# Clamped block additions, a square over three blocks, a second kind of group with seven products, and other tile starts

## The chip, the cores and the metric

The kernel runs on one core of one Trainium2 chip. The metric is the time of one execution on the device in microseconds (us). TensorE (PE in the profile) multiplies matrices; its weight loads are listed apart as PEld. VectorE (DVE) and ScalarE (ACT) work on elements, GpSimd (POOL) and SyncE (SP) issue DMA transfers here. The program gives each engine its own queue of instructions, in a fixed order.

## The reference

Two stages. Attention over channels: for each of 4 batches, q, k and v have 6080 tokens of 256 channels; q and k are normalised over the tokens, the 256 x 256 matrix of products of their channels goes through a softmax, and v is multiplied by it. Then a feed-forward block with 2048 hidden channels and the square of a relu:

```python
s = kn.transpose(0, 2, 1) @ qn / tau
a = softmax(s)                      # over the last axis
x = (v @ a).reshape(B * N, 256)
h = np.maximum(x @ w_in, 0.0)
return (h * h @ w_out).astype(np.float32)
```

## The kernel before

**Forms of the weights.** The softmax matrix is folded into `w_in` once per batch, so the main work is h = W.v and then out = w_out.h^2 for each block of tokens. Everything is held as a high and a low part (`_hi`, `_lo`) of the reduced type fp32r, and each product is three matmuls: hi with hi, hi with lo, lo with hi. The part that is streamed through the array is the "moving" operand: v and the parts of h^2.

**Blocks and groups.** A batch has 12 token blocks: ten of 512 tokens and two of 480, each used as two halves (256 or 240). The first two blocks of the run and the last one go another way. The 45 between them make 180 groups: four per block, j = 0 to 3, each with 512 of the hidden channels, that is two pairs of 256. `period(k)` writes out the work of group k. In a group both matrix products are done in the manner of Strassen and Winograd, on blocks of 2 x 2: seven block products instead of eight, with sums of blocks in place of the eighth.

- First product: `product` issues seven block products (42 matmuls) into the PSUM banks B2, H and C (`ps_b`, `ps_h`, `ps_c`). ScalarE copies or clamps them into the tile `x`, with blocks a0, a1, a3, a2 in this order, and VectorE adds what H and C hold to a1 and a3. The bank C starts as ScalarE's copy of B2, and PE then adds the product `C, S2` to it; so PE must wait for that copy.
- Square: before, a0 is clamped on the way out of PSUM and squared by ScalarE (`square`); a1 and a3 are added by VectorE and then clamped and squared by VectorE in one pass (`relu_squares`); a2 is clamped and squared by ScalarE.
- Sums: `first_sum`, `second_sum`, `third_sum` and `last_sum` on VectorE make the sums of blocks that the second product needs. `hi_A`/`lo_A` and `hi_S`/`lo_S` split them into parts (ScalarE makes the high part, VectorE the low one). The A tiles hold a1, a3, a2 and the S tiles (`s1`, `s2`; one name `s` in the profile) a0 with a1 and a3 with a2.
- Second product: `to_output` adds into the two output tiles `ps_o`, in three windows, `window_A`, `window_S(..., "S1")` and `window_S(..., "S2")`, of which the last falls into the period after next.

**Plain groups.** `plain(k)` tells whether the second pair of a group is done with eight block products instead of seven (its sums are then not taken, and each sum and its parts cover one pair instead of two). j=0 is always plain, j=2 and j=3 never after the first block, and j=1 is plain in all batches but the last: that is what `EARLY` and `LATER` say. For the seven products of a second pair, sums of blocks of `w_out` are needed, which `other_sums_of_w_out` makes for the j of EARLY around the first groups, and for those of LATER just before the last batch.

**Beside it.** While one batch runs, generators insert the next batch's attention at fixed points (`side("dve")`, `"pe"`, `"act"`, `"mid"`): one chunk of q and k per period, split into `qk_hi` and `qk_lo`, squared and added up, then the softmax, then the new forms of W. In the last batch there is nothing to insert. `v_step` splits the next token block's v at j=1 and j=2.

**Tiles.** The pools lay their tiles one behind another in SBUF. The two tiles `qk_lo` and `qk_hi` stand ahead of those of v (`v`, `v_hi`, `v_lo`) and of the S parts (`s_hi`, `s_lo`), and behind the A parts. Eight unused numbers at the end of each half make each of the two 64 bytes longer per partition than its content.

```python
EARLY = (2, 3)
LATER = (1,)
def plain(k):
    b, n, j = groups[k]
    return not (j in EARLY and (b, n) != order[OLD] or j in LATER and b == B - 1 and n >= LATER.index(j))
```

Of the kernel before, what the change touches and what calls it, by code (L numbers as in the profile page):

```python
# [7 lines left out]

F32 = mybir.dt.float32
# [5 lines left out]
ALU = mybir.AluOpType  # L15
# [15 lines left out]
def kernel(  # L31
# [484 lines left out]
    def attention(b):  # L516
# [21 lines left out]
        for c in range(c0, g.n):  # L538
            yield from until("act")
            if c > c0:  # L540
                g.squares(c - 1)
            p, jn, _ = g.q[c]
            hi = pool.tile([P, 2, J * C + 8], F32R, tag="qk_hi", name=f"qk_hi{b}_{c}", bufs=1)
            lo = pool.tile([P, 2, J * C + 8], F32R, tag="qk_lo", name=f"qk_lo{b}_{c}", bufs=1)
            hi, lo = (x[:, :, 0 : J * C].rearrange("p a (j c) -> p a j c", j=J) for x in (hi, lo))
            h_, l_, r_ = (x[:p, :, :jn, :] for x in (hi, lo, g.raws[c]))
            scalar.copy(h_, r_)
            yield
            yield from until("mid")
            add_and_load(c - 1)  # L550
            yield
            yield from until("dve")
            vector.tensor_sub(l_, r_, h_.bitcast(F32))
            yield
            yield from until("pe")
            for _ in g.products(c, [(hi, hi), (hi, lo), (lo, hi)]):
                pass
            yield
# [358 lines left out]
    BS = (B - 1,)  # L917
    EARLY = (2, 3)
    LATER = (1,)
    order = [(b, n) for b in range(B) for n in range(NB)]  # L920
# [37 lines left out]
    def half_of(k):  # L958
        return blocks[groups[k][1]][1] // 2
# [151 lines left out]

    def relu_squares(k):
        s = XG[k][:, :, a1 : a3 + 1, :]
        vector.scalar_tensor_tensor(s, s, 0.0, s, op0=ALU.max, op1=ALU.mult)

    def square(k, at):
        s = XG[k][:, :, at, :]
        scalar.activation(s, s, AF.Square)
# [76 lines left out]
    def period(k, before=nothing, w1=None, wa=None, w3=None):  # L1195
# [48 lines left out]
        product(k, H, S4, B22)  # L1244
        s = x[:, :, a1, :]
        vector.tensor_add(s, s, H[:, :, :half])
        if prev and not plain(k - 1):
            last_sum(k - 1)
        product(k, C, S3, T3)
        s = x[:, :, a3, :]  # L1250
        vector.tensor_add(s, s, C[:, :, :half])
        if prev:
            lo_S(k - 1, "S1")
            hi_S(k - 1, "S2")
        square(k, a0)
        relu_squares(k)
        if prev:
# [13 lines left out]
        evict_C21(k)  # L1271
        square(k, a2)
        if not after_copy(k):
# [217 lines left out]
```

## Time and profile before

| what | value |
|---|---|
| median of 3 runs | 2150.75 us (2150.54 to 2152.3) |
| profiled execution, from its first to its last instruction | 2150.0 us |
| granted TensorE clock | 1.000 |
| groups 0 to 178 | from 158.3 us to 2088.6 us of that execution |
| moved by DMA | 552.19 MB, mean 257 GB/s |

All instructions that the program issues through its recording wrapper carry one line number (L27), so the groups of the profile are told apart by the names of their tiles, out<-in, with the numbers left out: `ps_c<-v_hi,wf` is a product of the forms of W with v into the bank C. A row of the table of groups gives the count, the busy time and the mean duration of one. Durations on ScalarE and VectorE overlap a little: the next instruction starts about 0.1 us before the last one's recorded end.

The chain of work that ended last runs over TensorE for 90% of the span, over VectorE for 6% and over ScalarE for 1%.

### The profile page before, as it was taken

To read this page: it belongs to the slowest core of one execution; us is meant where nothing else is said; L and a number is where in the kernel's file an instruction comes from. 1 tells how busy PE (TensorE), PEld (TensorE's weight loads), DVE (VectorE), ACT (ScalarE), POOL (GpSimd) and SP (SyncE) were. 2 spreads that over 40 slices of the span, in tenths; PEclk is the share of its full clock that TensorE was granted. 3 is DMA by queue.
4 is the path that set the end of the run, shared out by engine and by line. 5 is a ranking of instruction groups with operands and counts; after the bars stand their busy time and mean duration, and the time that the engine had idled before them with its cause. 6 is when DMAs were issued, how large, how long until landed. Compare 5 with 4: busy or idle time off the path is not lost.

```text
span 2150.0 us, 44018 instructions
## 1 busy us (share of the span) xinstructions
PE 2139.5 (100%) x16990; PEld 2081.8 (97%) x16990; DVE 1973.7 (92%) x2739; ACT 1726.7 (80%) x2550; POOL 441.1 (21%) x561
## 2 busy tenths in 40 slices
PE   9999999999999999999999999999999999999999
PEld 8789999999999999999999999999999999999998
DVE  6899999999998999999999999999999999999993
ACT  5887888778878888877878888877887877877875
POOL 0000221212222221222122221221222222222221
PEclk9999999999999999999999999999999999999999
DMA  9777788879999988877999988887999788788783
GB/s 349 229 234 267 241 255 252 228 227 296 305 291 266 294 245 254 239 236 245 306 302 277 310 246 249 248 245 218 330 325 289 227 233 244 231 233 243 232 245 89
DMA packets 259986, 552.19 MB, mean 257 GB/s; under 512 B 27568, under 2 KB 120752, under 8 KB 259776
## 3 DMA queue, kind: packets, MB, share of 16 engines
q1 hardware_dynamic: 191488, 448.01, 61.8%
q0 software_dynamic: 68288, 101.35, 22.7%
q8 instruction: 134, 2.20, 0.4%
q14 instruction: 76, 0.62, 0.1%
HBM read 430.97 MB, written 63.70 MB: 230 GB/s over the span
## 4 chain that ended last, share of the span: by engine, by line
PE 90%; DVE 6%; DMA 1%; ACT 1%; issue 1%; SPq 0%; POOL 0%; DVEq 0%; ACTq 0%
PE ps_o L27 40%; PE ps_c L27 16%; PE ps_h L27 13%; PE ps_b L27 11%; PE gram L27 6%; DVE x L27 3%; PE ps_w L27 2%; DVE s_lo L27 1%; PE ps_o_m L27 1%; DVE A_lo L27 1%; DMA o<-o 1%; ACT x L27 1%; DMA qk<-in_q 0%; DVE v_lo L27 0%; DMA w_raw_hi<-in_w_in 0%
## 5 line engine op out<-in xcount | busy, mean ns | idle before, releaser
L27 DVE TENSOR_TENSOR s_lo<-x,s_hi 128x1024 fp32r<-128x1024 f32 (+1 forms) x384 | 463.4, 1207 | 37.8 <-ACT s_hi L27 37.7
L27 ACT CAST s_hi<-x 128x1024 fp32r<-128x1024 f32 (+1 forms) x384 | 400.8, 1044 | 96.7 <-DVE x L27 87.1
L27 PE MATMUL ps_c<-v_hi,wf 128*128 128x256 f32 (+1 forms) x2160 | 469.9, 281 | 3.3 <-DVE x L27 2.2
L27 POOL DMA_DIRECT2D o<-o x225 | 250.2, 1279 | 986.3 <-ACT o L27 612.0
L27 DVE TENSOR_TENSOR x<-x 128x512 f32<-128x512 f32 (+3 forms) x720 | 406.3, 564 | 15.7
L27 PEld LDWEIGHTS ps_c<-v_hi,wf 128*128 128x128 f32 x2160 | 369.1, 189 | 6.7 <-DVE x L27 3.5
L27 ACT CAST A_hi<-x 128x1024 fp32r<-128x1024 f32 (+3 forms) x360 | 247.2, 687 | 89.6 <-DVE x L27 81.4
L27 PE MATMUL ps_b<-v_hi,wf 128*128 128x256 f32 (+1 forms) x1440 | 311.8, 280 | 0.0
L27 PE MATMUL ps_h<-v_hi,wf 128*128 128x256 f32 (+1 forms) x1440 | 311.4, 279 | 0.0
L27 PE MATMUL ps_c<-v_lo,wf 128*128 128x256 f32 (+1 forms) x1080 | 301.9, 280 | 0.0
L27 DVE TENSOR_TENSOR A_lo<-x,A_hi 128x1024 fp32r<-128x1024 f32 (+3 forms) x360 | 275.5, 765 | 2.2 <-ACT A_hi L27 1.4
L27 ACT ACTIVATE x<-x 128x512 f32<-128x512 f32 (+3 forms) x384 | 251.8, 656 | 6.1
L27 PEld LDWEIGHTS ps_b<-v_hi,wf 128*128 128x128 f32 x1440 | 245.9, 189 | 0.1
L27 PEld LDWEIGHTS ps_h<-v_hi,wf 128*128 128x128 f32 x1440 | 245.8, 189 | 0.0
L27 ACT COPY x<-ps_c 128x512 f32<-128x512 f32 (+1 forms) x180 | 104.9, 583 | 168.3 <-PE ps_c L27 168.1
L27 DVE SCALAR_TENSOR_TENSOR x<-x 128x1024 f32<-128x1024 f32 (+1 forms) x180 | 217.3, 1207 | 0.0
L27 PE MATMUL ps_o<-s_hi,wo_hi 128*128 128x256 f32 (+3 forms) x1009 | 207.9, 296 | 0.5 <-ACT s_hi L27 0.5
L27 PE MATMUL ps_o<-s_lo,wo_hi 128*128 128x256 f32 (+3 forms) x1009 | 207.7, 296 | 0.1
L27 PE MATMUL ps_o<-s_hi,wo_lo 128*128 128x256 f32 (+3 forms) x1009 | 207.8, 296 | 0.0
L27 PEld LDWEIGHTS ps_c<-v_lo,wf 128*128 128x128 f32 x1080 | 203.8, 189 | 0.1
L27 PE MATMUL ps_h<-v_lo,wf 128*128 128x256 f32 (+1 forms) x720 | 201.5, 280 | 0.0
L27 PE MATMUL ps_b<-v_lo,wf 128*128 128x256 f32 (+1 forms) x720 | 201.2, 279 | 0.0
(165 smaller groups left out, 5113.5 us busy)
## 6 DMA issues: line engine op xcount, KB each, us to landing
wf<-wf_kept SPq DMA_DIRECT2D x360, 512.0 KB, 5.5
wf<-wf_kept SPq DMA_DIRECT2D x360, 384.0 KB, 5.0
o<-o POOLq DMA_DIRECT2D x114, 256.0 KB, 6.9
qk<-in_k SPq DMA_DIRECT2D x87, 256.0 KB, 5.1
qk<-in_q SPq DMA_DIRECT2D x87, 256.0 KB, 5.3
out_T<-o POOLq DMA_DIRECT2D x152, 128.0 KB, 5.3
v<-in_vT POOLq DMA_DIRECT2D x76, 128.0 KB, 3.8
v<-in_vT POOLq DMA_DIRECT2D x38, 256.0 KB, 4.1
```

What stands on the lines that cost most here:

```text
L27: return lambda *args, **kwargs: self.tc.keep_in_program_order(issue(*args, **kwargs))
```

## The change

It has three parts.

1. `EARLY = (1, 2, 3)`, `LATER = ()`: the groups j=1 of all blocks but the first use seven products for both pairs. 33 groups are concerned, those of batches 0 to 2; in batch 3 they did so already.
2. VectorE's two additions from PSUM clamp at zero in the same instruction (`add_relu`, a custom instruction that gives max(min(in0 + in1, s0), s1) with s0 infinite and s1 zero). VectorE's pass `relu_squares` goes, and ScalarE squares the blocks a0, a1 and a3 in one instruction.
3. The eight unused numbers in the `qk` tiles go. In the built program the v and S tiles then begin 128 bytes earlier, at multiples of 256 bytes instead of 128 past one; the A tiles stay where they were, at a multiple of 256.

```diff
@@ -5,6 +5,7 @@
 from concourse import mybir
 from concourse.masks import make_identity
 from concourse._compat import with_exitstack
+from concourse.dve_ops import TENSOR_ADD_SAT
 
 F32 = mybir.dt.float32
 F32R = mybir.dt.float32r
@@ -540,9 +541,9 @@
             if c > c0:
                 g.squares(c - 1)
             p, jn, _ = g.q[c]
-            hi = pool.tile([P, 2, J * C + 8], F32R, tag="qk_hi", name=f"qk_hi{b}_{c}", bufs=1)
-            lo = pool.tile([P, 2, J * C + 8], F32R, tag="qk_lo", name=f"qk_lo{b}_{c}", bufs=1)
-            hi, lo = (x[:, :, 0 : J * C].rearrange("p a (j c) -> p a j c", j=J) for x in (hi, lo))
+            hi = pool.tile([P, 2, J * C], F32R, tag="qk_hi", name=f"qk_hi{b}_{c}", bufs=1)
+            lo = pool.tile([P, 2, J * C], F32R, tag="qk_lo", name=f"qk_lo{b}_{c}", bufs=1)
+            hi, lo = (x.rearrange("p a (j c) -> p a j c", j=J) for x in (hi, lo))
             h_, l_, r_ = (x[:p, :, :jn, :] for x in (hi, lo, g.raws[c]))
             scalar.copy(h_, r_)
             yield
@@ -915,8 +916,8 @@
     OLD = 2
     ORD = 1
     BS = (B - 1,)
-    EARLY = (2, 3)
-    LATER = (1,)
+    EARLY = (1, 2, 3)
+    LATER = ()
     order = [(b, n) for b in range(B) for n in range(NB)]
     GPB = NPAIR // 2
     groups = [(b, n, j) for b, n in order[OLD:-1] for j in range(GPB)]
@@ -1109,12 +1110,12 @@
     def evict_C21(k):
         scalar.activation(XG[k][:, :, a2, :], C2.pop(k)[:, :, : half_of(k)], AF.Relu)
 
-    def relu_squares(k):
-        s = XG[k][:, :, a1 : a3 + 1, :]
-        vector.scalar_tensor_tensor(s, s, 0.0, s, op0=ALU.max, op1=ALU.mult)
-
-    def square(k, at):
+    def add_relu(k, at, ps):
         s = XG[k][:, :, at, :]
+        vector._custom_dve(TENSOR_ADD_SAT, out=s, in0=s, in1=ps[:, :, : half_of(k)], s0=float("inf"), s1=0.0)
+
+    def square(k, first, last):
+        s = XG[k][:, :, first : last + 1, :]
         scalar.activation(s, s, AF.Square)
 
     def sum_of(k, to, one, other, op):
@@ -1242,18 +1243,15 @@
         if w1 is None:
             copy_output(k - 2, 1)
         product(k, H, S4, B22)
-        s = x[:, :, a1, :]
-        vector.tensor_add(s, s, H[:, :, :half])
+        add_relu(k, a1, H)
         if prev and not plain(k - 1):
             last_sum(k - 1)
         product(k, C, S3, T3)
-        s = x[:, :, a3, :]
-        vector.tensor_add(s, s, C[:, :, :half])
+        add_relu(k, a3, C)
         if prev:
             lo_S(k - 1, "S1")
             hi_S(k - 1, "S2")
-        square(k, a0)
-        relu_squares(k)
+        square(k, a0, a3)
         if prev:
             lo_S(k - 1, "S2")
         side("pe")
@@ -1269,7 +1267,7 @@
         late_step()
         product(k, C, A22, T4)
         evict_C21(k)
-        square(k, a2)
+        square(k, a2, a2)
         if not after_copy(k):
             hi_A(k, late_A)
         (w3 or (lambda: window_S(k - 1, "S1")))()
```

**Where instructions stand.** Three places of the built programs, before and after. The first is ScalarE's queue around the end of group 53 (a j=1 group of batch 1 with a chunk beside it) and the start of group 54. `x53` is the tile of blocks, `qk2_10` a chunk, `v_hi1_4` the next token block's v. Before:

```order
L27 CAST s2_hi_52_9266<-x52_9059 128x1024
L27 ACTIVATE x53_9208<-x53_9208 128x2x256
L27 ACTIVATE qk2_10_8848<-qk2_10_8848 128x1024
L27 CAST qk_hi2_11_9285<-qk2_11_9013 128x2x512
L27 CAST v_hi1_4_9288<-v1_4_8852 128x1024
L27 CAST A_hi_53_9301<-x53_9208 128x512
L27 ACTIVATE x53_9208<-ps_c53_9195 128x2x256
L27 ACTIVATE x53_9208<-x53_9208 128x2x256
L27 CAST A_hi_53_9301<-x53_9208 128x256
L27 COPY ps_c54_9345<-ps_b54_9338 128x512
```

After:

```order
L28 CAST s2_hi_52_9224<-x52_9018 128x1024
L28 ACTIVATE x53_9166<-x53_9166 128x2x768
L28 ACTIVATE qk2_10_8817<-qk2_10_8817 128x1024
L28 CAST qk_hi2_11_9242<-qk2_11_8972 128x1024
L28 CAST v_hi1_4_9245<-v1_4_8821 128x1024
L28 CAST A_hi_53_9258<-x53_9166 128x2x512
L28 ACTIVATE x53_9166<-ps_c53_9153 128x2x256
L28 ACTIVATE x53_9166<-x53_9166 128x2x256
L28 CAST A_hi_53_9258<-x53_9166 128x2x256
L28 COPY ps_c54_9302<-ps_b54_9295 128x512
```

The square behind `s2_hi_52` covers 2 x 768 numbers per partition instead of 2 x 256, both casts to `A_hi_53` cover two pairs, and the copy into `ps_c54` still stands behind all of them.

The second is VectorE's queue in the same group, from its additions to the low parts and sums of `x53`. Before:

```order
L27 TENSOR_TENSOR x53_9208<-x53_9208,ps_h53_9197 128x2x256
L27 TENSOR_TENSOR x53_9208<-x53_9208,ps_c53_9195 128x2x256
L27 TENSOR_TENSOR s1_lo_52_9247<-x52_9059,s1_hi_52_9246 128x1024
L27 SCALAR_TENSOR_TENSOR x53_9208<-x53_9208 128x2x512
L27 TENSOR_TENSOR s2_lo_52_9267<-x52_9059,s2_hi_52_9266 128x1024
L27 TENSOR_TENSOR acc2_7771<-acc2_7771,qk2_10_8848 128x1024
L27 TENSOR_TENSOR v_lo1_4_9289<-v1_4_8852,v_hi1_4_9288 128x1024
L27 TENSOR_TENSOR A_lo_53_9302<-x53_9208,A_hi_53_9301 128x512
L27 TENSOR_TENSOR x53_9208<-x53_9208 128x256
L27 TENSOR_TENSOR A_lo_53_9302<-x53_9208,A_hi_53_9301 128x256
L27 TENSOR_TENSOR x53_9208<-x53_9208 128x256
```

After (ISA is the clamped addition):

```order
L28 ISA x53_9166<-x53_9166,ps_h53_9155 128x2x256
L28 ISA x53_9166<-x53_9166,ps_c53_9153 128x2x256
L28 TENSOR_TENSOR s1_lo_52_9205<-x52_9018,s1_hi_52_9204 128x1024
L28 TENSOR_TENSOR s2_lo_52_9225<-x52_9018,s2_hi_52_9224 128x1024
L28 TENSOR_TENSOR acc2_7738<-acc2_7738,qk2_10_8817 128x1024
L28 TENSOR_TENSOR v_lo1_4_9246<-v1_4_8821,v_hi1_4_9245 128x1024
L28 TENSOR_TENSOR A_lo_53_9259<-x53_9166,A_hi_53_9258 128x2x512
L28 TENSOR_TENSOR x53_9166<-x53_9166 128x2x256
L28 TENSOR_TENSOR A_lo_53_9259<-x53_9166,A_hi_53_9258 128x2x256
L28 TENSOR_TENSOR x53_9166<-x53_9166 128x2x256
```

The pass of 2 x 512 numbers is gone; `A_lo_53` and the sum between its parts are twice as wide.

The third is PE's queue at the window S1 of group 53 (12 rows of the second product, into the two output tiles). Before:

```order
L27 MATMUL ps_o1_3_1_9322<-s1_hi_53_9402,wS_hi_1231 128x256 x2
L27 MATMUL ps_o1_3_0_9291<-s1_hi_53_9402,wo_hi_109 128x512
L27 MATMUL ps_o1_3_0_9291<-s1_hi_53_9402,wo_hi_109 128x256
L27 MATMUL ps_o1_3_1_9322<-s1_hi_53_9402,wo_hi_109 128x256
L27 MATMUL ps_o1_3_1_9322<-s1_hi_53_9402,wS_lo_1232 128x256 x2
L27 MATMUL ps_o1_3_0_9291<-s1_hi_53_9402,wo_lo_110 128x512
L27 MATMUL ps_o1_3_0_9291<-s1_hi_53_9402,wo_lo_110 128x256
L27 MATMUL ps_o1_3_1_9322<-s1_hi_53_9402,wo_lo_110 128x256
L27 MATMUL ps_o1_3_1_9322<-s1_lo_53_9403,wS_hi_1231 128x256 x2
L27 MATMUL ps_o1_3_0_9291<-s1_lo_53_9403,wo_hi_109 128x512
L27 MATMUL ps_o1_3_0_9291<-s1_lo_53_9403,wo_hi_109 128x256
L27 MATMUL ps_o1_3_1_9322<-s1_lo_53_9403,wo_hi_109 128x256
```

After:

```order
L28 MATMUL ps_o1_3_1_9279<-s1_hi_53_9358,wS_hi_1231 128x256
L28 MATMUL ps_o1_3_1_9279<-s1_hi_53_9358,wo_hi_109 128x256
L28 MATMUL ps_o1_3_1_9279<-s1_hi_53_9358,wS_hi_1231 128x256
L28 MATMUL ps_o1_3_1_9279<-s1_hi_53_9358,wS_odd_hi_1902 128x256
L28 MATMUL ps_o1_3_1_9279<-s1_hi_53_9358,wS_lo_1232 128x256
L28 MATMUL ps_o1_3_1_9279<-s1_hi_53_9358,wo_lo_110 128x256
L28 MATMUL ps_o1_3_1_9279<-s1_hi_53_9358,wS_lo_1232 128x256
L28 MATMUL ps_o1_3_1_9279<-s1_hi_53_9358,wS_odd_lo_1903 128x256
L28 MATMUL ps_o1_3_1_9279<-s1_lo_53_9359,wS_hi_1231 128x256
L28 MATMUL ps_o1_3_1_9279<-s1_lo_53_9359,wo_hi_109 128x256
L28 MATMUL ps_o1_3_1_9279<-s1_lo_53_9359,wS_hi_1231 128x256
L28 MATMUL ps_o1_3_1_9279<-s1_lo_53_9359,wS_odd_hi_1902 128x256
```

The three matmuls of 512 columns and the products into the other output tile are gone; `wS_odd` holds the sums of `w_out` for the second pair. In the window A of this group there are 18 matmuls instead of 9, in S1 12 instead of 15, in S2 12 instead of 18.

## The prediction

> **What bounds the kernel now.** I read the page's first part, then the table of TensorE's waits, then busy times by stage (columns: stretch, its length, busy us and count of PE, PEld, DVE, ACT and POOL, granted clock, DMA share, GB/s).
>
> ```profile
> PE 2139.5 (100%) x16990; PEld 2081.8 (97%) x16990; DVE 1973.7 (92%) x2739; ACT 1726.7 (80%) x2550; POOL 441.1 (21%) x561
> ...
> PE ps_c L27 <- DVE x L27: 2.2, 5, 0.8
> PE ps_c L27 <- ACT ps_c L27: 0.8, 2, 0.6
> ...
> 687.80:871.20 183.40, 183.40 (x1538) 182.37 (x1537) 177.38 (x231) 156.06 (x225) 40.91 (x52) 1.00 0.88 268
> 1697.50:2059.70 362.20, 362.20 (x3027) 361.01 (x3026) 343.02 (x451) 287.60 (x433) 85.72 (x109) 1.00 0.82 237
> ```
>
> TensorE has no gap in either stretch, at full clock, and waits for the block sums and copies only about 3 us in the whole run. So the time is the number of matmuls times their spacing. The first stretch also prepares the next batch's attention ("chunks"); there VectorE is busy 177.38 of 183.40 us (97%) and ScalarE 156.06 (85%). A change to these two pays only where TensorE waits, and costs as soon as TensorE comes to wait for them.
>
> **Part 1: groups j=1 by seven products.** Per group and pass, TensorE then issues 42 output matmuls of one width where it issued 39 of one width and 3 of two. The group's wide form against its narrow one (columns: count, busy us, mean ns):
>
> ```profile
> L27 PE MATMUL ps_o<-s_hi,wo_hi 128*128 128x512 f32 x132 | 47.1, 396 | 0.5 <-ACT s_hi L27 0.5
> L27 PE MATMUL ps_o<-s_hi,wo_hi 128*128 128x256 f32 x728 | 143.2, 280 | 0.0
> ```
>
> One wide matmul costs 396 - 280 = 116 ns more. 33 groups change: 27 with halves of 256 tokens, 6 with 240. 81 x 0.116 + 18 x 0.116 x 240/256 = 9.4 + 2.0 = **11.3 us off TensorE's queue**, on the path. The sums of `w_out` for j=1 move from the last batch to groups 3 and 4; I cost that at nothing net, since as many instructions leave the other place, and keep 1 us each way. The price is in the parts of the sums, which now cover two pairs:
>
> ```profile
> L27 ACT CAST A_hi<-x 128x1024 fp32r<-128x1024 f32 x84 | 88.5, 1053 | 46.9 <-DVE x L27 45.9 <-PE ps_c L27 1.0
> L27 ACT CAST A_hi<-x 128x512 fp32r<-128x512 f32 x152 | 94.4, 621 | 24.5 <-DVE x L27 22.7
> L27 ACT CAST A_hi<-x 128x256 fp32r<-128x256 f32 x68 | 27.7, 407 | 2.2
> L27 ACT ACTIVATE x<-x 128x512 f32<-128x512 f32 x304 | 192.8, 634 | 4.9
> L27 ACT ACTIVATE qk<-qk 128x1024 f32<-128x1024 f32 x63 | 66.5, 1055 | 0.0
> L27 DVE SCALAR_TENSOR_TENSOR x<-x 128x1024 f32<-128x1024 f32 x152 | 185.1, 1218 | 0.0
> L27 DVE TENSOR_TENSOR x<-x,ps_c 128x512 f32<-128x512 f32 x152 | 103.7, 682 | 0.0
> L27 DVE TENSOR_TENSOR A_lo<-x,A_hi 128x1024 fp32r<-128x1024 f32 x84 | 102.3, 1218 | 1.9 <-ACT A_hi L27 1.4
> L27 DVE TENSOR_TENSOR A_lo<-x,A_hi 128x512 fp32r<-128x512 f32 x152 | 104.0, 684 | 0.0
> L27 DVE TENSOR_TENSOR x<-x 128x512 f32<-128x512 f32 x336 | 231.1, 688 | 7.5
> L27 DVE TENSOR_TENSOR x<-x 128x256 f32<-128x256 f32 x272 | 114.8, 422 | 5.5
> ```
>
> ScalarE: (1053 - 621) + (621 - 407) = **0.65 us more per changed group**. VectorE: one low part from 512 to 1024 elements (1218 - 684) and five passes from 256 to 512 (688 - 422 each), 1.9 us more; I cost that at nothing, because part 2 frees 4 x 1.2 us in the same four groups.
>
> **Part 2: the clamp and the square.** VectorE loses one pass of 1218 ns in each of 180 groups, some 217 us. ScalarE's square of one block becomes one of three: 1055 - 634 = 0.42 us per 512 more elements, so **+0.84 us in every group**. The Trainium skill ("ScalarE: Activation LUTs", Rules for kernel authors) advises VectorE for max and mul, up to about 3x faster per element, in bf16. For these fp32 elements the rows disagree: 1218 ns there against 1055 here.
>
> The clamped add is not in this trace. It reads the same two operands, so I see no reason for it to be cheaper than 682 ns. The two-operation pass over 1024 elements took 1218 ns, and so does the subtraction that makes A_lo: a second operation was free. That is the nearest row and I take 0; the upper end is a second pass over 512 elements, 1218 - 682 = +0.54 us.
>
> Who hides the 0.84 us? Timeline rows (start us, length, what): first one of the last batch, then VectorE's add and ScalarE around group 53 (j=1) with PE's first product behind ScalarE's copy in group 54.
>
> ```profile
> 1888.39 1.05 ACT L27 CAST A_hi<-x 128x1024 fp32r<-128x1024 f32 x1 [1.34 <-DVE x L27]
> ...
> 751.06 0.68 DVE L27 TENSOR_TENSOR x<-x,ps_c 128x512 f32<-128x512 f32 x1
> ...
> 748.76 0.59 ACT L27 COPY x<-ps_c 128x512 f32<-128x512 f32 x1 [0.69 <-PE ps_c L27]
> ...
> 752.52 0.65 ACT L27 ACTIVATE x<-x 128x512 f32<-128x512 f32 x1
> 753.05 1.07 ACT L27 ACTIVATE qk<-qk 128x1024 f32<-128x1024 f32 x1
> 754.00 1.06 ACT L27 CAST qk_hi<-qk 128x1024 fp32r<-128x1024 f32 x1
> 754.94 1.06 ACT L27 CAST v_hi<-v 128x1024 fp32r<-128x1024 f32 x1
> 755.88 0.64 ACT L27 CAST A_hi<-x 128x512 fp32r<-128x512 f32 x1
> ...
> 757.71 0.41 ACT L27 CAST A_hi<-x 128x256 fp32r<-128x256 f32 x1
> 758.02 0.58 ACT L27 COPY ps_c<-ps_b 128x512 f32<-128x512 f32 x1
> ...
> 759.44 0.28 PE L27 MATMUL ps_c<-v_hi,wf 128*128 128x256 f32 x1
> ```
>
> In the last batch A_hi waits 1.34 us for VectorE's clamping pass. That wait goes, the 0.84 us stand in its place, and nothing is late. Where chunks are in flight, their rows (qk) fill that time, and the cover is missing: from 748.76 to 758.60 ScalarE never rests. Then its copy into `ps_c` must end before PE adds a product there at 759.44. Slack 0.84 us. Added on this stretch: 0.84 + 0.65 = 1.49 us. How close the two may come shows where PE waited already:
>
> ```profile
> 225.89 0.58 ACT L27 COPY ps_c<-ps_b 128x512 f32<-128x512 f32 x1
> 226.52 0.39 PE L27 MATMUL ps_c<-v_hi,wf 128*128 128x256 f32 x1 [0.60 <-ACT ps_c L27]
> ...
> 581.02 0.55 ACT L27 COPY ps_c<-ps_b 128x480 f32<-128x480 f32 x1
> 581.63 0.38 PE L27 MATMUL ps_c<-v_hi,wf 128*128 128x240 f32 x1
> ...
> 1380.18 0.58 ACT L27 COPY ps_c<-ps_b 128x512 f32<-128x512 f32 x1
> 1381.59 0.28 PE L27 MATMUL ps_c<-v_hi,wf 128*128 128x256 f32 x1
> ```
>
> 226.52 - 226.47 = 0.05. So 1.49 - (0.84 - 0.05) = 0.70 us of **new wait on TensorE**, 0.77 when its own 10 us before it are 0.7% shorter (part 3). Group 54 is one of 13 such places (every fourth group with chunks in flight, the last at 1381.59, slack 0.83): 10.0 us. In three groups that build weights, as at 581.63, slack is 0.06 already: 3 x 1.37 (480 elements for 512) = 4.1 us. At the first converted group, where 226.52 shows PE waiting before the change, and the two behind it: 3.0 us. Eight more of these places, with slack of 0.9 to 1.3, I put at 0.3 each: 2.4. In sum **+19.5 us**. What is queued behind the late copy (the copy of `ps_h`, halves of v, the copy back from `ps_c`) keeps its slack, because PE is late by as much. VectorE's relief removes at most its waits shown above: **-2.2 us**.
>
> **Part 3: tile starts.** By the program, tiles of v and of the S sums begin 128 bytes past a multiple of 256, those of the A sums on one. Removing 64 bytes from each of two tiles ahead puts all on one. Busy PE time of one tile alone, A_hi and then the products that read v, in each of the two stages:
>
> ```profile
> 687.80:871.20 183.40, 19.45 (x144) 1.00 0.88 268
> 687.80:871.20 183.40, 86.87 (x672) 1.00 0.88 268
> 1697.50:2059.70 362.20, 50.06 (x378) 1.00 0.82 237
> 1697.50:2059.70 362.20, 197.85 (x1513) 1.00 0.82 237
> ```
>
> A run of n matmuls is busy (n - 1) spacings and one duration of 0.28. A_hi has one run per group, v three. A_hi: (19.45 - 16 x 0.28) / 128 = 117.0 ns, and (50.06 - 36 x 0.28) / 342 = 116.9. v: (86.87 - 48 x 0.28) / 624 = 117.7, and (197.85 - 108 x 0.28) / 1405 = 119.3. Same weights and output bank for A and S, same place in the period for A and the v products around it; what sets A apart is where it starts. If v and S come down to A: 28 sets of four groups at 276 matmuls x 0.7 ns = 5.4 us, 10 in the last batch at 273 x 2.4 = 6.6: **-12.0 us** (the seven sets with halves of 240 tokens have mixed starts before and after: 0). The lower end is nothing; a loss is excluded, as tiles at the new start run fastest today. Between these ends A's rows are nearest, so I take -12.0. The Trainium skill ("SBUF — State Buffer", SBUF: two separate sides) says reads pay per 16-byte line and that PE never waits on another engine. 128 is a multiple of 16, so by that the move brings nothing; it is the first rival, and the step from 116.9 to 119.3 speaks against it.
>
> **Sum.** The profiled execution spans 2150.0 us. 2150.0 - 11.3 - 2.2 - 12.0 + 19.5 = 2144.0. The median of the runs, 2150.75, is 0.75 above that span: **2145**.
>
> **Rivals.**
> - *Starts don't matter*, and ScalarE's lateness outweighs the matmuls saved: 2145 + 12 = **2157**. It decides from the point where the saving is half of what I took, some 0.6 ns a matmul: there the time is back at the old one. For it: the difference is 1%, and v itself differs by stage at one address. Against: A holds 117 in both stages. Chance 0.22.
> - *ScalarE is not late*: the wider square or the freed VectorE closes the 0.7 us. Then 2145 - 19.5 = **2125.5**. For it: ScalarE is only 85% busy where chunks run. Against: it is in order, without rest over the 9.8 us that matter. Chance 0.10.
> - *The clamped add takes two passes*, +0.54 us each. Behind group 53 the last add ends at 751.74 + 1.08 = 752.82 and holds the square by 0.3; behind j=3 groups S_hi waits for a sum queued after the first add, 0.54 late with no slack left. 13 x 0.84 = 11 us and perhaps half of it again elsewhere: **2162**. For it: an instruction of another kind; against: the two-operation row. Chance 0.08.
>
> **How the numbers follow.** The forecast holds 0.60. The range, 2133 to 2162, takes in the first rival and stalls between 10 and 24 us, and leaves out the second rival and some of the third. A difference under 0.2% (4.3 us) can hardly be told from none. The forecast lies near that bound: 0.36 faster, 0.21 the same, 0.03 slower; the first rival gives 0.07 the same and 0.15 slower, the second 0.10 faster, the third 0.08 slower. Together 0.46, 0.28, 0.26.
>
> **What would show it.** Right: 117 ns spacing for v and S in both stages; TensorE waiting some 0.7 us for ScalarE's copy into `ps_c` one group behind each j=1 group where chunks run, and no wait in the last batch; clamped adds near 682 ns; a square near 1476 ns. Wrong: v still at 119 in the last batch (first rival), no such waits (second), adds over 1.1 us (third).

## The result and the profile after

| | before | after |
|---|---|---|
| median of 4 runs, us | 2150.85 (2150.54 to 2152.3) | 2166.53 (2165.44 to 2167.94) |
| profiled execution, us | 2150.0 | 2165.8 |
| ratio to before | | 1.0067, 95% interval 1.0055 to 1.0079 |

The kernel became slower by 15.7 us, where 5.75 us less was forecast; the time lies 4.5 us above the range. The first part of the page of after (columns as in the prediction), and the engines of the chain that ended last:

```profile
PE 2132.2 (98%) x16990; PEld 2066.8 (95%) x16990; DVE 1842.7 (85%) x2559; ACT 1893.0 (87%) x2550; POOL 440.6 (20%) x561
...
PE 71%; ACT 18%; DVE 4%; issue 3%; DMA 2%; SPq 1%; ACTq 0%; DVEq 0%
```

VectorE is relieved as foreseen (92% to 85%). ScalarE, with 1% of the chain before, now has 18%. The table of waits of after (total, times, longest, in us) says for what:

```profile
PE ps_c L28 <- ACT ps_c L28: 18.2, 31, 1.8
PE ps_b L28 <- DMA wf<-wf_kept: 3.1, 2, 1.9
PE gram L28 <- DVE qk_lo L28: 2.9, 3, 1.7
...
ACT s_hi L28 <- DVE x L28: 105.8, 146, 1.7
```

TensorE waits 18.2 us for ScalarE's copy into `ps_c`, where it waited 0.8 before. A wait shows too short here by up to 0.16 us, because the record of the matmul ahead (0.28) reaches beyond the spacing (0.117); so stages are better compared by their length. Lateness "by starts", used further down, is read from the start times instead: how much later than usual a matmul starts after the one ahead of it (usual is the median for that width, and only more than 0.06 us counts), added up over groups 4 to 175. "At j=2" then means ahead of the products into the bank C in groups j=2, without groups 48 to 51, and so for the other j. The busy times of the new instructions, in the table of groups of after:

```profile
L28 DVE CUSTOM_DVE_ANT_0 x<-x,ps_h 128x512 f32<-128x512 f32 x152 | 104.2, 685 | 73.2 <-PE ps_h L28 73.0
L28 DVE CUSTOM_DVE_ANT_0 x<-x,ps_c 128x512 f32<-128x512 f32 x152 | 103.4, 680 | 0.0
L28 ACT ACTIVATE x<-x 128x1536 f32<-128x1536 f32 x152 | 226.5, 1490 | 2.0 <-DVE x L28 2.0
```

So the new instructions cost about what was taken (682 and 1476), and the loss is in waits. Lengths of stages in us, from the first product of one group to that of another, from starts in the two timelines rounded to 0.1 us:

| groups | what runs beside | before | after | difference |
|---|---|---|---|---|
| 4 to 11 | first chunks, first forms of W, sums of `w_out` | 95.2 | 102.8 | +7.6 |
| 12 to 47 | the rest of batch 0 and one block with chunks | 393.6 | 396.3 | +2.7 |
| 48 to 51 | chunks | 45.9 | 50.8 | +4.9 |
| 52 to 91 | chunks, then forms of W | 438.7 | 443.4 | +4.7 |
| 92 to 111 | chunks in all five blocks | 229.3 | 234.1 | +4.8 |
| 112 to 131 | forms of W | 215.5 | 214.9 | -0.6 |
| 132 to 175 | last batch, nothing | 442.5 | 434.4 | -8.1 |

The last batch gained the 6.6 that was forecast for the tile starts and 1.5 more; `clamp`, below, shows that part 2 alone is worth 1.9 there (440.6 for 442.5). The others lost. The row 92 to 111 is the cleanest place to look: busy times by stage, of before and then of after (columns as in the prediction).

```profile
1172.40:1401.70 229.30, 229.30 (x1923) 228.03 (x1922) 219.82 (x287) 195.05 (x282) 50.06 (x63) 1.00 0.87 260
```

```profile
1192.00:1426.10 234.10, 230.38 (x1922) 226.84 (x1921) 208.51 (x267) 214.17 (x281) 49.72 (x62) 1.00 0.85 255
```

TensorE's records had no gap there and have 3.7 us now. ScalarE went from 85% of the stage to 91% (214.17 of 234.10), while VectorE still has 89% (96% before): both are nearly full. The timeline of after around groups 53 (j=1), 54 and 55, with ScalarE, VectorE and TensorE together (start, length, what, wait ahead of it):

```profile
767.69 1.50 ACT L28 ACTIVATE x<-x 128x1536 f32<-128x1536 f32 x1
...
771.91 1.07 ACT L28 CAST A_hi<-x 128x1024 fp32r<-128x1024 f32 x1
...
774.16 0.62 ACT L28 CAST A_hi<-x 128x512 fp32r<-128x512 f32 x1
774.69 0.58 ACT L28 COPY ps_c<-ps_b 128x512 f32<-128x512 f32 x1
...
775.32 0.38 PE L28 MATMUL ps_c<-v_hi,wf 128*128 128x256 f32 x1 [0.60 <-ACT ps_c L28]
...
778.00 0.68 DVE L28 CUSTOM_DVE_ANT_0 x<-x,ps_h 128x512 f32<-128x512 f32 x1
778.60 0.68 DVE L28 TENSOR_TENSOR x<-x 128x512 f32<-128x512 f32 x1
...
779.32 1.05 ACT L28 CAST s_hi<-x 128x1024 fp32r<-128x1024 f32 x1 [0.87 <-DVE x L28]
...
786.31 0.58 ACT L28 COPY ps_c<-ps_b 128x512 f32<-128x512 f32 x1
786.55 0.28 PE L28 MATMUL ps_o<-s_lo,wS_odd_hi 128*128 128x256 f32 x1
786.95 0.38 PE L28 MATMUL ps_c<-v_hi,wf 128*128 128x256 f32 x1
```

The wait of group 54 is the one forecast: 0.60 + 0.16 = 0.76 us. The rest was not. At 779.32 ScalarE waits 0.87 us for a sum (the row at 778.60, `last_sum` of group 53). For a plain group this sum stood ahead of both additions from PSUM; group 53 isn't plain any more, so by the code it stands behind the addition from `ps_h`. ScalarE therefore doesn't recover. Its next copy into `ps_c` ends at 786.89, and TensorE, due at 786.55 + 0.12, starts at 786.95, 0.28 us late.

### The profile page after: what moved, and what is told of

The parts are those of the page before. It is cut to its first block, busy times and chain, and to the rows that moved or that the text cites. A ratio compares the mean times of both kernels' runs of the same rounds, so it can differ in the third digit from the quotient of the medians.

```text
span 2165.8 us, 44008 instructions
## 1 busy us (share of the span) xinstructions
PE 2132.2 (98%) x16990; PEld 2066.8 (95%) x16990; DVE 1842.7 (85%) x2559; ACT 1893.0 (87%) x2550; POOL 440.6 (20%) x561
## 3 DMA queue, kind: packets, MB, share of 16 engines
q0 software_dynamic: 68288, 101.35, 22.1%
## 4 chain that ended last, share of the span: by engine, by line
PE 71%; ACT 18%; DVE 4%; issue 3%; DMA 2%; SPq 1%; ACTq 0%; DVEq 0%
PE ps_o L28 30%; PE ps_c L28 15%; PE ps_h L28 11%; PE ps_b L28 8%; ACT x L28 6%; PE gram L28 5%; ACT A_hi L28 2%; ACT s_hi L28 2%; ACT qk L28 2%; ACT qk_hi L28 2%; PE ps_w L28 2%; DVE x L28 2%; ACT ps_c L28 2%; ACT v_hi L28 1%; DMA wf<-wf_kept 1%
## 5 line engine op out<-in xcount | busy, mean ns | idle before, releaser
L28 PE MATMUL ps_c<-v_hi,wf 128*128 128x256 f32 (+1 forms) x2160 | 472.5, 283 | 20.8 <-ACT ps_c L28 18.2
L28 DVE TENSOR_TENSOR s_lo<-x,s_hi 128x1024 fp32r<-128x1024 f32 (+1 forms) x384 | 452.5, 1207 | 41.3 <-ACT s_hi L28 39.4
L28 DVE TENSOR_TENSOR x<-x 128x512 f32<-128x512 f32 (+3 forms) x720 | 440.7, 612 | 15.0 <-ACT A_hi L28 0.5
L28 ACT ACTIVATE x<-x 128x1536 f32<-128x1536 f32 (+5 forms) x384 | 404.3, 1053 | 8.1 <-DVE x L28 2.0
L28 DVE TENSOR_TENSOR A_lo<-x,A_hi 128x1024 fp32r<-128x1024 f32 (+3 forms) x360 | 301.8, 838 | 39.3 <-ACT A_hi L28 39.0
L28 ACT CAST A_hi<-x 128x1024 fp32r<-128x1024 f32 (+3 forms) x360 | 267.9, 744 | 6.4
L28 PE MATMUL ps_o<-s_hi,wo_hi 128*128 128x256 f32 (+2 forms) x844 | 181.1, 295 | 0.5 <-ACT s_hi L28 0.5
L28 PE MATMUL ps_o<-s_hi,wo_lo 128*128 128x256 f32 (+2 forms) x844 | 181.1, 295 | 0.0
L28 PE MATMUL ps_o<-s_lo,wo_hi 128*128 128x256 f32 (+2 forms) x844 | 180.6, 294 | 0.1
L28 DVE CUSTOM_DVE_ANT_0 x<-x,ps_h 128x512 f32<-128x512 f32 x152 | 104.2, 685 | 73.2 <-PE ps_h L28 73.0
```

What stands on the lines that cost most here:

```text
L28: return lambda *args, **kwargs: self.tc.keep_in_program_order(issue(*args, **kwargs))
```

## The experiments

The theory from here on: *parts 1 and 2 together make ScalarE late at its copies into `ps_c`; waits of ScalarE for VectorE's reordered sum carry the lateness from j=2 to j=3 and j=0; the sums of `w_out` crowd the first blocks.* The rivals: one part alone does it; part 3 brought nothing or harm; late transfers. All times are medians of fresh runs, each beside runs of the kernel before on the same chip (medians 2151.4 to 2151.9); in brackets the ratio to it with its 95% interval. The kernel before had 2150.85 beside the changed kernel, so a difference to the changed kernel's 2166.53 is uncertain by about 1 us for the chip alone.

### Each part alone, and parts 1 and 2 together

`starts` (the diff's tile part only):

> Part 3 alone on the kernel before (the qk tiles without their eight unused numbers). Theory (the starts are worth 0.7 ns a matmul where chunks run and 2.4 in the last batch): 12 us less, 2139, ratio 0.9944. Rival (starts don't matter, what became faster in the changed kernel came from elsewhere): 2150 to 2151. A third possibility, that the tiles of q and k lose at their new start what v gains: 63 chunks x 12 matmuls x some 1.3 ns = 1 us, so 2140.

Measured: 2141.99 (0.9957, 0.9945 to 0.9970).

`seven` (`EARLY = (1, 2, 3)`, `LATER = ()` only):

> Part 1 alone on the kernel before (groups j=1 by seven products, VectorE still clamps and squares). Theory: 11.3 us leave TensorE's queue, but VectorE, 97% busy where chunks run, gets 1.9 us more in each of 27 groups, and its reordered last sum holds S_hi: about half of the gain goes, 2143 to 2150, with some 6 us lost in the first two blocks where the sums of w_out are made. Rival (the loss of the changed kernel comes from the wider square alone): 2139 to 2141.

Measured: 2162.19 (1.0045, 1.0033 to 1.0058).

`clamp` (`add_relu` and the square of three blocks only):

> Part 2 alone on the kernel before (clamped additions, ScalarE squares three blocks). Theory (ScalarE is late only where the 0.84 us meet the 0.65 of part 1 and the reordered last sum): about no change, 2148 to 2154. Rival (the wider square alone makes ScalarE late at every copy into ps_c where chunks run): 16 blocks x 1 us and more, 2165 and above.

Measured: 2155.80 (1.0019, 1.0010 to 1.0027).

`seven_clamp` (the change without its tile part):

> The changed kernel without part 3 (tiles start where they did before). Theory (part 3 saves some 12 us less what it loses where TensorE waits anyway): 10 to 12 us more than the changed kernel, 2176 to 2179. Rival (starts don't matter): 2166 to 2167.

Measured: 2174.32 (1.0106, 1.0090 to 1.0121).

Part 3 helps, by 9.9 us alone and by 7.8 on top of the other two (6.7 when each kernel is held against its own runs of before); its first rival falls. Part 1 alone costs 10.3 us, worse than both my theory and its rival. Part 2 alone costs 3.9, near my theory and far from the rival. Together they cost 22.4, so 8.2 us exist only in combination. Why part 1 costs alone is seen in the busy times of `seven` for groups 92 to 111, and in ScalarE's waits there, of before and of `seven`:

```profile
1181.00:1411.30 230.30, 229.40 (x1922) 227.35 (x1921) 226.03 (x286) 196.79 (x280) 50.87 (x65) 1.00 0.86 261
```

```profile
ACT s_hi L27 <- DVE x L27: 7.1, 10, 0.7
...
ACT s_hi L27 <- DVE x L27: 20.7, 19, 1.4
```

VectorE is busy for 226.03 of 230.30 us (98%). In the same stretch ScalarE's waits for it before S_hi are 20.7 us, against 7.1 before the change: the 1.9 us that the prediction costed at nothing meet an engine without room here, and part 2, which makes the room, fills ScalarE. How much of the 20.7 comes from the 1.9 us and how much from the last sum, which part 1 moves as well, was not run apart. Part 1 without part 2 but with the better starts:

> Parts 1 and 3 without part 2 (VectorE clamps and squares). Theory (part 1 costs 10 us by itself, part 3 saves 8 to 10, and neither needs the other): 2152 to 2154, some 13 us below the changed kernel, so that part 2 costs that much where j=1 is converted. Rival (with VectorE left at 97% the faster matmuls of part 3 only lengthen waits): 2158 or more.

Measured: 2153.46 (1.0015, 1.0005 to 1.0024), 13 us below the changed kernel. So part 2, meant to make room for part 1, costs more than that room was worth.

That part 3 works as a matter of where tiles start is read from busy PE time of one tile, A_hi and then v, in the two stages of the prediction, here of `starts_lag` (part 3 with one more edit, shown further down, that moves two loads):

```profile
687.80:871.20 183.40, 19.46 (x144) 1.00 0.88 266
1700.00:2060.00 360.00, 49.99 (x378) 1.00 0.83 240
...
687.80:871.20 183.40, 86.75 (x677) 1.00 0.88 266
1700.00:2060.00 360.00, 195.98 (x1530) 1.00 0.83 240
```

By the prediction's formula v now takes about (86.75 - 48 x 0.28) / 629 = 116.6 ns and (195.98 - 109 x 0.28) / 1421 = 116.4, where it took 117.7 and 119.3. A, which didn't move, stays at 117.0 and 116.7. By the two rules of the Trainium skill that the prediction weighed ("SBUF — State Buffer", SBUF: two separate sides), that reads pay per 16-byte line and that PE never waits on another engine, v would have stayed as it was. The measurement decides: for these matmuls the two together don't give the time, and which of them falls short isn't shown.

### The order of the last sum

```diff
         if prev:
             third_sum(k - 1)
-            if plain(k - 1):
+            if plain(k - 1) or groups[k - 1][2] == 1:
                 last_sum(k - 1)
...
         add_relu(k, a1, H)
-        if prev and not plain(k - 1):
+        if prev and not plain(k - 1) and groups[k - 1][2] != 1:
             last_sum(k - 1)
```

This is `sum_early1`; in `sum_early` the sum comes first in all groups.

> The changed kernel with one move: behind a group j=1, the last sum stands right behind the third sum in VectorE's queue, as before the change, instead of behind the addition from ps_h. Theory (ScalarE's lateness is carried on because its high part of S2 waits 0.87 us for that sum in the period of j=2): the waits at the copy into ps_c at j=3, 0.28 us a block, go, and part of those at j=0; 15 blocks x 0.3 to 0.5, so 4 to 7 us less, 2160 to 2162. Rival (the high part would only run up to the next wait, or the sum delays VectorE's addition by as much): 2166 to 2167.

Measured: 2160.55 (1.0044, 1.0030 to 1.0057), 6.0 us less.

> The changed kernel with the last sum right behind the third sum in all groups. Theory (every wait of ScalarE for this sum, 0.7 to 0.9 us a period, is lateness that ends at the copy into ps_c): waits at j=3 and j=0 go and those at j=2 shrink, 15 blocks x 0.6 to 1.0, 2151 to 2158. Rival (VectorE's additions from PSUM, 0.7 us later, hold up TensorE's banks instead): 2166 or more.

Measured: 2155.56 (1.0018, 1.0009 to 1.0027), 11.0 us less. Busy times of `sum_early` for groups 92 to 111:

```profile
1184.30:1416.70 232.40, 229.35 (x1922) 226.75 (x1921) 209.76 (x267) 215.68 (x281) 49.84 (x62) 1.00 0.85 258
```

And its timeline at groups 54 and 55, the place shown above:

```profile
768.87 0.58 ACT L28 COPY ps_c<-ps_b 128x512 f32<-128x512 f32 x1
769.51 0.39 PE L28 MATMUL ps_c<-v_hi,wf 128*128 128x256 f32 x1 [0.61 <-ACT ps_c L28]
...
773.02 1.05 ACT L28 CAST s_hi<-x 128x1024 fp32r<-128x1024 f32 x1 [0.39 <-DVE x L28]
...
780.31 0.58 ACT L28 COPY ps_c<-ps_b 128x512 f32<-128x512 f32 x1
780.73 0.28 PE L28 MATMUL ps_o<-s_lo,wS_odd_hi 128*128 128x256 f32 x1
780.94 0.39 PE L28 MATMUL ps_c<-v_hi,wf 128*128 128x256 f32 x1
```

The carried part shrinks: the distance to the first product behind the copy falls from 0.40 to 0.21 us in group 55, and the stage from 234.1 to 232.4. The wait of group 54 is untouched (0.61). By starts, TensorE's lateness of 7.6 us in that stage has three parts: 4.4 at j=2, 1.9 that the sum carried on to j=3 and j=0, and 1.4 there that stay with the sum moved; less what parts 1 and 3 save, that makes the 4.8. The 1.7 us are 0.34 a block, some 4 us for the eleven blocks with a chunk beside every group. Groups 48 to 51 gave 2.5 us (48.3 for 50.8); most of the rest came from blocks that build W, which I had not expected to be held by this. The same move in the kernel before was not run; there TensorE's records have only some 6 us of waits in all.

### ScalarE's work ahead of the copy

```diff
-    BS = (B - 1,)
+    BS = tuple(range(B))
```

> The changed kernel with the high part of the last A block behind the copy into ps_c in all batches, not only in the last (BS holds all four). Theory (what the change loses where chunks run is TensorE's wait for that copy, 1.2 us a block of four groups): with 0.62 us of ScalarE's work out of the way the waits at j=3 and j=0 go and the one at j=2 falls from 0.76 to about 0.15, 15 blocks x 1.0, 2151 to 2154. Rival (the high part then comes too late for the A products, whose low part VectorE makes from it, and TensorE waits there): 2164 or more.

Measured: 2160.84 (1.0045, 1.0033 to 1.0058): 5.7 us less, neither theory. Its busy times for groups 92 to 111, and the row of S_hi in the waits of that stretch, of after and then of `late_A`:

```profile
1185.00:1420.90 235.90, 232.68 (x1923) 227.66 (x1922) 208.37 (x267) 212.17 (x282) 50.32 (x64) 1.00 0.84 253
```

```profile
ACT s_hi L28 <- DVE x L28: 12.1, 15, 0.9
...
ACT s_hi L28 <- DVE x L28: 22.1, 15, 1.7
```

Where chunks run it got worse (235.9 for 234.1): the same 15 waits of S_hi for VectorE grew to 22.1 us from 12.1. By starts, over the whole run, the lateness at j=2 halves (10.4 us for 21.1) and that at j=1 rises (7.4 for 1.9). So making one copy earlier by putting work behind it mostly shifts the lateness. What it gained came from the other blocks. My expectation that the copy alone was short of time fell here.

`mix` takes `sum_early` and gives the clamp and the square of a1 and a3 back to VectorE in groups j=1 only:

```diff
+    def relu_squares(k):
+        s = XG[k][:, :, a1 : a3 + 1, :]
+        vector.scalar_tensor_tensor(s, s, 0.0, s, op0=ALU.max, op1=ALU.mult)
...
     def add_relu(k, at, ps):
         s = XG[k][:, :, at, :]
+        if groups[k][2] == 1:
+            vector.tensor_add(s, s, ps[:, :, : half_of(k)])
+            return
...
-        square(k, a0, a3)
+        square(k, a0, a0 if j == 1 else a3)
+        if j == 1:
+            relu_squares(k)
```

> The kernel sum_early (the changed kernel with the last sum early in all groups) in which the groups j=1 add without a clamp and VectorE clamps and squares their a1 and a3 as before the change. Theory (the wait of 0.77 us at j=2 is ScalarE's: 0.84 us of wider square behind 0.65 us of wider parts, met by 0.84 of slack): with the 0.84 gone the wait at j=2 goes, 15 blocks x 0.7 = 10 us less than sum_early, 2144 to 2147. Rival (ScalarE has no time left in these blocks at all, so that the wait moves to j=3 or j=0; or VectorE is late with its pass): 2152 to 2156.

Measured: 2142.67 (0.9960, 0.9948 to 0.9973), 12.9 us less than `sum_early`. Busy times of groups 92 to 111, and the same place in the timeline of `mix`:

```profile
1174.00:1402.10 228.10, 228.10 (x1923) 226.49 (x1922) 214.85 (x272) 211.41 (x282) 50.12 (x63) 1.00 0.87 263
```

```profile
762.05 0.58 ACT L28 COPY ps_c<-ps_b 128x512 f32<-128x512 f32 x1
...
762.77 0.30 PE L28 MATMUL ps_c<-v_hi,wf 128*128 128x256 f32 x1
```

The copy ends at 762.63, 0.14 us before TensorE's product at 762.77; TensorE's records show no gap in the whole stage (by starts 1.4 us are left, at j=3 and j=0), and the stage is 1.2 us shorter than before the change. VectorE has 94% and ScalarE 93%. One pass of 1.2 us in every fourth group, moved back, is worth 12.9 us, and by starts the lateness at j=2 falls from 21.6 us in `sum_early` to 3.0: it was ScalarE's wide square behind the wide parts.

### The first blocks

In `sums_later` the sums of `w_out` for j=1 are made after the others (from group 7 on) and group 5 stays plain:

```diff
-            while now["k"] < base + (GPB * i if base else 0) + j + 2:
+            while now["k"] < (GPB + 3 if j == 1 else j + 2):
...
-    EARLY = (1, 2, 3)
+    EARLY = (2, 3, 1)
...
-        return not (j in EARLY and (b, n) != order[OLD] or j in LATER and b == B - 1 and n >= LATER.index(j))
+        return not (j in EARLY and (b, n) not in order[OLD : OLD + (2 if j == 1 else 1)] or j in LATER and b == B - 1 and n >= LATER.index(j))
```

> The changed kernel with the sums of w_out for j=1 made after those for j=2 and j=3, from group 7 on, and the group j=1 of the second block (group 5) still by eight products. Theory (the sums moved ahead crowd groups 3 to 5, where the first chunks run: 5.9 us in groups 4 to 7): 3 to 5 us less, 2161 to 2163. Rival (the loss there is that of the converted group itself and comes one block later): 2166 to 2167.

Measured: 2164.47 (1.0059, 1.0046 to 1.0072), 2.1 us less. And `from1`:

```diff
-    EARLY = (1, 2, 3)
-    LATER = ()
+    EARLY = (2, 3)
+    LATER = (1,)
...
-        return not (j in EARLY and (b, n) != order[OLD] or j in LATER and b == B - 1 and n >= LATER.index(j))
+        return not (j in EARLY and (b, n) != order[OLD] or j in LATER and b >= 1)
...
-    LATE_SUMS = groups.index((B - 1, 0, 0)) - GPB
+    LATE_SUMS = groups.index((1, 0, 0)) - GPB
...
-        if g == LATE_SUMS:
-            forming.append(other_sums_of_w_out(LATER, g))
+        if g == LATE_SUMS + 3:
+            forming.append(other_sums_of_w_out(LATER, LATE_SUMS))
```

> The changed kernel with the groups j=1 by seven products from the second batch on only; their sums of w_out are made between the chunks of the two batches (groups 39 and 40). Theory (the changed kernel loses 8 us in groups 4 to 11 because the sums and the first converted groups fall among the first chunks and the first forms of W): 5 to 7 us less than the changed kernel, 2159 to 2162. Rival (those blocks are slow for another reason, the wider square for one): 2165 to 2167.

Measured: 2163.14 (1.0059, 1.0045 to 1.0072), 3.4 us less.

TensorE's waits in groups 4 to 11, of after and then of `sums_later`:

```profile
PE ps_c L28 <- ACT ps_c L28: 5.4, 4, 1.8
PE gram L28 <- DVE qk_lo L28: 2.9, 3, 1.7
```

```profile
PE ps_c L28 <- ACT ps_c L28: 5.5, 5, 1.5
PE gram L28 <- DVE qk_lo L28: 0.3, 1, 0.3
```

The sums explain the waits for VectorE (2.9 to 0.3); they are instructions of VectorE put where it makes `qk_lo`. The waits for ScalarE stay. With `from1` the two blocks take 97.5 us instead of 102.8, but the stages from group 92 on take 6.1 us more. The ratios of both kernels, 1.0059, lie within the interval of the changed kernel, so that their gain shows in the stages and not in the medians. `mix` with the edit of `from1`, and then with that of `sums_later`:

> mix and from1 together. If both theories hold, the two savings add up: 2137 to 2141, below the kernel with part 3 alone (2142). If ScalarE's time in these blocks is used up whatever the order, 2146 or more.

Measured: 2142.57 (0.9961, 0.9948 to 0.9973), no less than `mix`. Its waits show where the saving went, the sums of j=1 in the other place:

```profile
PE ps_o L28 <- ACT wo_hi L28: 4.2, 1, 4.2
```

> mix with the sums of w_out for j=1 behind those for j=2 and j=3 and group 5 by eight products (as in sums_later). Theory (what is left of the loss in groups 4 to 11 comes from these sums and that group, 2.7 us less in sums_later): 2139.5 to 2140.5, below part 3 alone. Rival (mix has relieved ScalarE there already, so that the order of the sums changes nothing): 2142 to 2143.

Measured: 2140.94 (0.9945, 0.9933 to 0.9958). That is the theory's direction; 1.7 us are within the spread of either kernel's runs.

### A transfer that lands late

In groups 48 to 51 the profile of after shows a loss that the neighbours don't have: 4.9 us, where five blocks like it lost 1.0 each. POOL's queue, VectorE and TensorE in its timeline:

```profile
702.29 1.07 POOL L28 DMA_DIRECT2D out_T<-o  x2 [1.23 <-DMA o<-o]
703.35 0.92 POOL L28 DMA_DIRECT2D acc<-qk  x1
713.01 0.87 POOL L28 DMA_DIRECT2D acc<-qk  x1 [8.74 <-ACT o L28]
...
722.12 0.36 PE L28 MATMUL ps_b<-v_hi,wf 128*128 128x256 f32 x1 [1.87 <-DMA wf<-wf_kept]
...
722.25 1.23 DVE L28 TENSOR_TENSOR acc<-acc,qk 128x1024 f32<-128x1024 f32 x1 [4.15 <-DMA acc<-qk]
```

The squares of the second to sixth chunk of a batch are added up by adding transfers on POOL's queue (`acc<-qk`), one after the other into the same tile; the later ones by VectorE. The first transfer shown stands behind the block's output and is issued 5.6 us after the first product of group 48 (2.7 us before the change, first row below), and two things end late behind it: SP's next load into that raw buffer, behind which the forms of W wait in SP's queue, and VectorE's first addition into the same tile, 4.15 us (0.35 before, second row).

```profile
690.47 0.92 POOL L27 DMA_DIRECT2D acc<-qk  x1
...
709.44 1.23 DVE L27 TENSOR_TENSOR acc<-acc,qk 128x1024 f32<-128x1024 f32 x1 [0.35 <-DMA acc<-qk]
```

I took the first for the cause and had the load issued one chunk later from the third batch on:

```diff
             g.add_squares(c)
+            c -= b > 1
             if c0 <= c and c + ahead < g.n:
```

> The changed kernel in which, from the third batch's chunks on, the load of q and k into a raw buffer is issued one chunk later, so that it no longer waits in SP's queue for the adding transfer out of the same buffer. Theory (in groups 48 to 51 the forms of W stand behind that load in SP's queue, come late, and cost TensorE 3.9 us): 3 to 4 us less than the changed kernel, 2162.5 to 2163.5. Rival (the load then comes too late itself, or the late forms have another reason): 2166 or more.

Measured: 2168.30 (1.0077, 1.0064 to 1.0089), no less than the changed kernel.

> Part 3 alone with the same later load. Theory (of the 12 us of part 3, 2 are given back where faster matmuls meet late forms of W: 3.6 and 2.5 us at two places of the profile of part 3 alone): 2139 to 2140. Rival (late forms in one profile are chance, and the 12 us were too many): 2142.

Measured: 2142.24 (0.9955, 0.9941 to 0.9969), the median of `starts`.

> mix_later with the later load. If both hold: 2137 to 2138.5; if neither, 2142.5.

Measured: 2139.99 (0.9949, 0.9937 to 0.9962), not to be told from `mix_later`. In `after_lag` TensorE waits for no form of W any more in these groups, and they still take 50.3 us (50.8): the theory falls. What stayed is VectorE's wait. So, last, VectorE adds up the fifth and sixth chunk itself:

```diff
-                if self.b and c < HEAD:
+                if self.b and c < HEAD - 2 * (self.b > 1):
                     pool_engine.dma_start(a, sq, accum_op=ALU.add)
```

> The changed kernel in which, in batches 2 and 3 of 0 to 3, the squares of the fifth and sixth chunk are added up by VectorE instead of by an adding transfer on POOL's queue. Theory (in groups 48 to 51 the last adding transfer, held up behind the block's output, lands late, and VectorE's next addition waits 4.2 us for it, 5.3 in after_lag, where no form of W was late and the loss was the same): the wait goes, 3 to 4 us less than the changed kernel, 2162.5 to 2163.5. Rival (VectorE, 89% busy there, loses with 2 x 1.2 us more work in each of two batches what it gains; or the late forms decide after all): 2165.5 or more.

Measured: 2164.06 (1.0060, 1.0046 to 1.0073), 2.5 us less than the changed kernel, though the intervals of the two ratios overlap. VectorE's waits between 690 and 740 us, the longest of each kernel: after, `after_lag`, `after_vec`.

```profile
DVE acc L28 <- DMA acc<-qk: 4.2, 1, 4.2
```

```profile
DVE acc L28 <- DMA acc<-qk: 5.3, 1, 5.3
```

```profile
DVE acc L28 <- ACT qk L28: 2.3, 3, 1.1
```

The wait is gone and groups 48 to 51 take 46.8 us, as long as the blocks of groups 92 to 111: in these profiles this transfer was the cause. The profiles of the other kernels agree: where this addition waits 2.7 us or more for the transfer (nine kernels with the changed one), these groups take 47.7 to 50.9 us; in the others they take 45.6 to 47.4, except in `mix` (48.2 without such a wait). The same with `mix_later`:

> mix_later with the same edit. Theory: groups 48 to 51 lost 2.3 us in the profile of mix_later; 2 us less, 2139. Rival (VectorE is 94% busy in mix and the added work comes back as a wait): 2141 or more.

Measured: 2139.60 (0.9941, 0.9929 to 0.9954), the lowest median of all; 1.3 us below `mix_later`, within the spread of the runs. In its profile VectorE waits 3.2 us for the last transfer that is left, ahead of its first addition. Why the block's output in front of the transfer lands later than before the change stays open. Part 3 alone shows the same loss, and `seven_clamp`, without part 3, has no such wait (46.8 us): the profile of `starts`, 2145.2 us, has a wait of 3.3 us there, that of `starts_lag` (2137.4 us) 1.8, at the same median.

## Why the prediction was wrong

The gains were about right and the new waits were half of what came. From the span: 15.8 us more, although part 1 was to save 11.3 and part 3 saved about 12; so some 39 us of waits, where 19.5 were forecast. By starts, over groups 4 to 175, the lateness is 12.1 us before and 51.9 after, 39.8 more.

- *What bounds the kernel*: right. TensorE's records have no gap where the kernel is fast (`mix`, 228.10 of 228.10), and the time is lost where they have.
- *Part 1, 11.3 us off TensorE's queue*: the matmuls left, but the gain is had only where VectorE and ScalarE keep up. Groups 20 to 43 took 256.1 us before, 255.8 after and 252.0 in `mix`, where part 1 and part 3 were to bring 3.2.
- *Part 1, VectorE's 1.9 us at nothing because part 2 makes room*: not tested by itself. Without part 2, in `seven`, part 1 costs 10.3 us; with it VectorE has room (89%), and it is the order of its queue that costs (below). *The moved sums of `w_out` at nothing*: wrong, they cost 2 to 3 in the first blocks.
- *Part 2, prices*: right. 685 and 680 ns for the clamped additions, 1490 for the square; the 1.34 us wait in the last batch went, and the records of TensorE have one wait of 0.4 us left there. The third rival falls. *VectorE's relief, 2.2*: right, TensorE's waits for VectorE's `x` are gone from the table.
- *Part 2, a new wait of 0.70 to 0.77 us behind each j=1 group*: right at its place (0.76), and shown to be ScalarE's by `mix`. By starts the lateness at j=2 rose by 19.5 us, from 1.6 to 21.1, just the sum that the prediction had for all its new waits; that it agrees to the tenth is luck, as the single terms don't all (3.0 for the first converted groups, 2.0 measured at j=2 in groups 4 to 11).
- *"What is queued behind the late copy keeps its slack, because PE is late by as much"*: **this step failed.** I followed ScalarE's queue to TensorE and stopped there. One period on, S_hi waits for a sum that the conversion of j=1 itself had moved behind the addition from `ps_h` in VectorE's queue; the lateness goes on to j=3 and j=0, which the prediction had at nothing: by starts 10.8 us more at j=3 and 2.1 at j=0. Putting j=1's sum first (`sum_early1`) gives back 6.0 us and, in its profile, halves the lateness at j=3 (5.2 us) while j=2 stays late by 21.6; putting the sum first in all groups gives back 11.0. The half at j=3 that stays is not explained by a run; `seven` alone has 6.5 us there, and `mix` 8.3.
- *First converted groups, 3.0 us*: too small. Groups 4 to 11 lost 7.6 in all, although parts 1 and 3 were to shorten them by 1.1. By starts 2.7 of it lie at the products of q and k, 2.5 at j=3 and 2.0 at j=2. `clamp` alone loses 2.4 there (97.6 for 95.2 us) and `seven` 3.6 (98.8).
- *Part 3, 12.0 us*: right in the spacing (116.4 to 116.6) and, in the profiled execution of `starts_lag`, its fastest, in size: 2150.0 - 2137.4 = 12.6. The medians give 9.5 and 9.9, a fifth less; in the profile of `starts` some of it is given back at the late transfer. The first rival, that starts don't matter, falls.
- The adding transfer that lands late in groups 48 to 51, 3.9 us more than in their neighbours, had no term.

Together: by starts the 39.8 us are 19.5 at j=2, which were forecast in sum; 10.8 at j=3 and 2.1 at j=0, which the failed step left out; 5.5 in groups 48 to 51 and 2.8 at the products of q and k, which had no term; and 0.9 less at j=1. Half of what was missing can be given back by one instruction's place in VectorE's queue; why the rest is late was not run apart.

## What to carry to other kernels

When an instruction becomes late, follow its lateness through all the queues for a whole round of the loop, not to the first engine that waits: the question is where the late engine gets its time back, and whether the change itself has taken that place away. Work moved from one nearly full engine to another nearly full one is best moved in the groups that have room; here one pass given back in every fourth group was worth 12.9 us, and the mixed kernel (`mix_later_vec`, 2139.6) beats both kernels, though hardly the tile starts alone (2142.0), the smallest part of the change. And run the parts of a change alone: two of the three were losses that the third partly hid.

## What the runs showed of the hardware that was not expected

A start at a multiple of 256 bytes is not the faster one everywhere. Before the change, by the program, two of the three kinds of products of q and k streamed qk_hi from 64 bytes past such a multiple, against weights from 32 or 96 past one; the third streams qk_lo from a multiple, against weights from 96 past one. With part 3 all begin on a multiple, and the products became slower. Busy PE time of the tile `gram` over five blocks with chunks, of before and of `starts_lag`:

```profile
1172.40:1401.70 229.30, 31.52 (x240) 1.00 0.87 260
```

```profile
1170.00:1399.00 229.00, 31.86 (x240) 1.00 0.87 260
```

That is 0.34 / 240 = 1.4 ns a matmul more, or 63 chunks x 12 x 1.4 = 1.1 us in the run, against 1.1 to 2.9 ns gained by each product that reads v. The third kind became slower too, from 118.0 to 118.9 ns from start to start, though only its loaded operand moved. So the streamed start alone doesn't explain it; the two weren't run apart. VectorE's clamped addition, a custom instruction with two more operations, cost the same as the plain one (680 to 685 ns against 682).
